# Attention with a routed mixture of experts on one core: the place of the output evictions on the queues of ScalarE and VectorE

## The chip, the cores and the metric

The kernel runs on one core of one Trainium2 chip. A core has five engines with a queue of instructions each: TensorE (PE in the profile, its weight loads PEld), VectorE (DVE), ScalarE (ACT), GpSimd (POOL) and SyncE (SP), which here only issues transfers. The metric is the time of one execution in microseconds (us); the time before is the median of three runs.

## The reference

Causal attention with a decaying bias over 8 batches, 8 heads, 576 positions and head size 64; then each of the 4608 tokens goes to the one of 8 experts with the highest logit, through two matrices with a ReLU between, and is scaled by its gate.

```python
scores = scale * np.matmul(q, k.transpose(0, 1, 3, 2))
...
attn = np.exp(scores)
attn = attn / (np.sum(attn, axis=-1, keepdims=True) + 1e-09)
...
x = np.ascontiguousarray(attn_out.transpose(0, 2, 1, 3)).reshape(B * S, H * D)
...
logits = x @ w_gate + modality_bias[modality_id]
e_idx = np.argmax(logits, axis=1)
...
for e in range(E):
    mask = e_idx == e
    ...
    h = np.maximum(x[mask] @ w1[e], 0.0)
    out[mask] = gate_w[mask, None] * (h @ w2[e])
```

Here x is 4608 x 512, w1 of one expert 512 x 1024, w2 of one expert 1024 x 512, all in 32-bit floats.

## The kernel before, in words

The first half of the time is the attention (class Attn), whose output rows are scattered into one list for each expert (Route). The second half is the experts (class Moe), in blocks. A block is 256 rows of one expert's list. There are 18 such blocks (6 from the table t2, 12 from t3); I count them from 0. After them come two short pieces of 64 rows each (`two`), and a loop over what is left, which the diff does not touch.

A block (`block`, then `second`) has these parts.

- Its expert's weights come as 8 tiles of 128 x 1024, four of w1 and four of w2, by SP into raw buffers (`fetch`, tiles wraw and wrbw; the buffers are few, and a transfer into one waits for its last reader). `parts` converts a raw tile: a cast to the matmul's reduced 32-bit type on ScalarE (L975), which is the high part, and on VectorE the raw value less that high part (L976), which is the low part. The converted tiles are called wca, wcb and wcc, by the pool that they come from. High and low parts are multiplied in three passes (`PASS1`, `PASS`), to keep the precision.
- Its rows come as tile xr, and `xt` turns them: two transposes on VectorE (L1067), a cast on ScalarE (L1069) and a subtraction on VectorE (L1070) for each half of xT. This is issued between the two halves of the block before.
- First half: 96 matmuls of 256 columns into hp (L1117), with four times a ReLU on ScalarE (L1119) and a subtraction on VectorE (L1120) that make hT.
- Second half: 48 matmuls of 512 columns into the two banks y (L1092).
- Eviction: y[0] times the gate on ScalarE (L1102), y[1] times the gate on VectorE (L1100), each into a tile ys, and a scatter of ys to the output's rows by POOL (L1103). Both evictions wait for the block's last matmuls.

While a block runs, `step` issues the fetches and conversions of the next block's eight tiles, one at a time: two before the block begins, and then one after each of the four steps of the first half and of the second. Which row stands where on an engine's queue is not the order of the code alone: the tile context's scheduler orders the rows of each engine, and `issue_after(i)` tells it that what follows must stand behind instruction i. Each engine then works its queue off in order. So a row that waits at the head of a queue holds up all rows behind it.

Of the kernel before, what the change touches and what calls it, by code (L numbers as in the profile page):

```python
# [7 lines left out]
F32 = mybir.dt.float32  # L8
# [3 lines left out]
AF = mybir.ActivationFunctionType  # L12
ALU = mybir.AluOpType
# [560 lines left out]
N2 = 6  # L574
WGP = (1, 2, 3, 4, 8)
PRI = 300
PRI2 = 900
PRI3 = 200
SCS = 5, 5, 4, 4
# [331 lines left out]
class Moe:  # L911
    def __init__(self, ctx, tc, R, w1, w2, ident, out):
        self.nc, self.tc, self.R, self.w1, self.w2, self.ident, self.out = tc.nc, tc, R, w1, w2, ident, out
        self.wa = ctx.enter_context(tc.tile_pool(name="mwa", bufs=1))
        self.wb = None
        self.n = 0
        self.last = [None] * 4
        self.hold = None
        self.late, self.stop = None, 1 << 30
        self.back = ()  # L920
        self.er = None

    def open(self, ctx):
        tc = self.tc
        self.my, self.mx, self.wr, self.wb, self.mp = (
            ctx.enter_context(self.tc.tile_pool(name=n, bufs=2, reuse_waits="tile")) for n in ("mys", "mmx", "mwr", "mwb", "mm"))
        self.R.tb = ctx.enter_context(tc.tile_pool(name="mtb", bufs=1, reuse_waits="tile"))
        self.ps = ctx.enter_context(tc.tile_pool(name="mps", bufs=2, space=PSUM, reuse_waits="tile"))
# [28 lines left out]
    def parts(self, raw, d, n, j, w=None):  # L957
        nc = self.nc
        m = (n - self.NA) % (self.NA + self.NB + self.NC)
        if w is not None:  # L960
            pass
        elif n < self.NA or self.NB <= m < self.NB + self.NA:
            w = self.wa.tile([P, 2, 1024], F32R, name="wca", bufs=self.NA)
        elif m < self.NB:
            w = self.wb.tile([P, 2, 1024], F32R, name="wcb", bufs=self.NB)
        else:
            w = self.wc.tile([P, 2, 1024], F32R, name=f"wcc{(m - self.NB - self.NA + 2) % self.NC}")
        n += 1
        with ExitStack() as after:
            for i in self.tr[1:] if 4 < n <= 8 else self.back:  # L970
                after.enter_context(self.tc.issue_after(i.ins))
            if n <= self.NA:
                nc.gpsimd.tensor_scalar(w[:, 0], raw, 1.0, 1.0, ALU.mult, ALU.mult)
            else:
                nc.scalar.copy(w[:, 0], raw)  # L975
            (nc.gpsimd if n in WGP else nc.vector).tensor_tensor(w[:, 1], raw, w[:, 0].bitcast(F32), ALU.subtract)  # L976
        return w, d

    def regs(self, tb, b):
# [103 lines left out]
    PASS = ((0, 0), (0, 1), (1, 0))  # L1083
    PASS1 = ((0, 0), (1, 0), (0, 1))

    def second(self, W, xg, oi, hT):
        nc = self.nc
        y = [self.ps.tile([P, 512], F32, name="y") for _ in range(2)]
        for f in range(8):
            for u in range(2):  # L1090
                for i, (a, c) in enumerate(self.PASS):
                    self.last[0] = nc.tensor.matmul(y[u], hT[:, a, f, P * u:P * u + P], W[4 + f // 2][:, c, 512 * (f % 2):512 * (f % 2) + 512],  # L1092
                                                    start=f == 0 and i == 0, stop=f == 7 and i == 2)
            if f % 2:
                self.step()
        for u in range(2):
            ys = self.my.tile([P, 512], F32, name="ys", bufs=3)
            gate = xg[1][:, u, 0:1]
            if u:
                self.last[1] = nc.vector.tensor_scalar(ys, y[u], gate, None, ALU.mult)  # L1100
            else:
                self.last[3] = nc.scalar.activation(ys, y[u], AF.Copy, scale=gate)  # L1102
            self.last[2] = nc.gpsimd.indirect_dma_start(  # L1103
                out=self.out, out_offset=bass.IndirectOffsetOnAxis(ap=oi[:, u:u + 1], axis=0),
                in_=ys, in_offset=None, bounds_check=4607, oob_is_err=False)

    def block(self, W, xg, oi, xT, mid):

        nc = self.nc
        hT = self.mp.tile([P, 2, 8, 256], F32R, name="hT", bufs=1)  # L1110
        for m in range(4):
            hp = self.ps.tile([P, 2, 256], F32, name="hp")
            for u in range(2):
                f = P * (2 * m + u)
                for k in range(4):
                    for i, (a, c) in enumerate(self.PASS1):
                        nc.tensor.matmul(hp[:, u], W[k][:, a, f:f + P], xT[:, c, k], start=k == 0 and i == 0, stop=k == 3 and i == 2)  # L1117
            hs = hT[:, 0, 2 * m:2 * m + 2]
            hi = nc.scalar.activation(hs, hp, AF.Relu)  # L1119
            lo = nc.vector.scalar_tensor_tensor(hT[:, 1, 2 * m:2 * m + 2], hp, 0.0, hs.bitcast(F32), ALU.max, ALU.subtract)  # L1120
            if self.late is not None:
                self.back = (hi, lo)
            self.step()
        mid()
        self.second(W, xg, oi, hT)

    def quads(self, xg, k):
        return xg[:, 0, :32].rearrange("p d h r -> p (d h r)")[:, k::4]
# [91 lines left out]
    def sums(self, o, W, parts, scale=1.0, after=()):  # L1220

        nc = self.nc
        n = len(parts)
        for i, (x, k, c0) in enumerate(parts):
            def low():
                nc.tensor.matmul(o[:64], x[:, :64], W[k][:, 1, c0:c0 + 512], start=False, stop=False)
            if i:
                low()
            self.last[0] = nc.tensor.matmul(o, x, W[k][:, 0, c0:c0 + 512], start=i == 0, stop=i == n - 1)
            if not i:  # L1230
                low()
        lo = self.wc.tile([64, 512], F32, name="ql", bufs=2)
        with ExitStack() as behind:
            for i in after:
                behind.enter_context(self.tc.issue_after(i.ins))
            self.last[3] = nc.scalar.activation(lo, o[64:], AF.Copy, scale=scale)
        return lo
# [70 lines left out]
    def run(self, lst, early=False, then=None, routed=None, half=None):  # L1308

        def pre(k):  # L1310
            tb, b, nu = getattr(self.R, lst[k][0]), lst[k][1], lst[k][2]
            if nu == 0:
                e, r = zip(*(self.regs(tb, b + q) for q in range(2)))
                self.stop = self.n + 14
            else:
                e, r = self.er if early and k == 0 else self.regs(tb, b)
            if early and k == 0:
                (xg, oi), x = self.first
            else:
                xg, oi = self.gather(tb, b, r, nu)  # L1320
                x = self.xt(xg, nu) if k == 0 else None
            W, self.more = self.weights(e, self.have if early and k == 0 else ()) if nu else self.weights2(e)
            for _ in range(0 if self.late is not None else 2 if k else 8):
                next(self.more, 0)
            return W, xg, oi, x
        with (self.tc.high_priority(offset=PRI) if early else ExitStack()):
            *nxt, nx = pre(0)
        if routed is not None:
            routed()
        for k in range(len(lst)):  # L1330
            cur, xT = nxt, nx
            if then is not None:
                then(k)
            if early and k == 0:
                self.stop = 8 + self.NB + 2
            if k + 1 < len(lst):
                *nxt, _ = pre(k + 1)
            def mid():
                if half is not None:
                    half(k)  # L1340
                if k + 1 < len(lst):
                    nxts.append(self.xt(nxt[1], lst[k + 1][2]))
            nxts = []
            with (self.tc.high_priority(offset=PRI) if early and k == 0 else ExitStack()):
                (self.two, self.quarter, self.block)[lst[k][2]](*cur, xT, mid)
            if early and k == 0:
                self.late, self.stop = self.more, 1 << 30
            else:
                while self.n < self.stop and next(self.more, 0) is None:
                    pass  # L1350
            self.back = ()
            nx = nxts[0] if nxts else None


def build(tc, qkv, s, mid, wg, mb, w1, w2, out):
    nc = tc.nc
    with ExitStack() as ctx:
# [36 lines left out]
        with ExitStack() as mctx:  # L1394
# [3 lines left out]
            def routed():  # L1398
                with ExitStack() as after:
                    for i in M.tr[1:]:  # L1400
                        after.enter_context(tc.issue_after(i.ins))
                    with tc.high_priority(offset=PRI2):
                        while next(bg[0][0]) != "mm":
# [64 lines left out]
```

## Time and profile before

| | us |
|---|---|
| three runs | 816.35, 816.20, 814.23; median 816.2 |
| profiled execution | 815.56 |
| its span, first to last instruction | 813.8 |
| mean granted clock of TensorE | 0.994 of full |
| first eviction of an expert block, last one | 400.35, 791.40 |

All rows are of the profiled execution, counted from the start of its span. A row of the timeline gives start, length, engine, line, operation, what is written from what is read, the tile sizes and how many; in a bracket, how long the engine had waited before it and for what. The waits are put down to what came last by the profile.

### The profile page before, as it was taken

What the parts mean: (1) busy time and instruction counts of PE and PEld (TensorE: products, weight loads), DVE (VectorE), ACT (ScalarE), POOL (GpSimd) and SP (SyncE); (2) the same over time, 40 slices, a digit from 0 to 9 for tenths busy, and PEclk for the clock granted to TensorE, in tenths of its full rate; (3) what the DMA queues carried; (4) which work ended last, traced back from release to release, by engine and by line L of the source; (5) the groups of instructions that cost most, each with busy time, mean ns of one, the idle gap of its engine ahead of it and who ended that gap; (6) DMA issues with size and microseconds to landing.
All of it is one profiled execution on the core that took longest, in us unless ns stands there. A gap on an engine that the chain in (4) does not pass through costs nothing. (4 is left out here: it accounts for less than half of the span.)

```text
span 813.8 us, 16745 instructions
## 1 busy us (share of the span) xinstructions
PE 796.1 (98%) x5548; PEld 681.1 (84%) x5548; DVE 577.9 (71%) x1441; ACT 526.4 (65%) x1194; POOL 364.2 (45%) x385
## 2 busy tenths in 40 slices
PE   7999999999999999999999999899999999999997
PEld 6778888888878888887888998798889998988884
DVE  7666667667666677768779695677787776777664
ACT  6788778887878788785554544555555555455553
POOL 8959777988699867984601001100000010001000
PEclk9999999999999999999999999999999999999999
DMA  7665556776567665749888977577778777778750
GB/s 240 175 197 184 181 185 196 230 236 194 166 186 215 220 178 171 233 151 256 292 278 279 321 253 278 177 253 231 249 254 260 252 242 254 262 256 249 257 182 29
DMA packets 88133, 181.16 MB, mean 223 GB/s; under 512 B 13753, under 2 KB 33081, under 8 KB 87918
## 3 DMA queue, kind: packets, MB, share of 16 engines
q1 hardware_dynamic: 82206, 160.03, 62.6%
q0 software_dynamic: 5840, 20.06, 6.3%
q8 instruction: 44, 0.72, 0.4%
q14 instruction: 43, 0.35, 0.1%
HBM read 143.59 MB, written 26.80 MB: 209 GB/s over the span
## 5 line engine op out<-in xcount | busy, mean ns | idle before, releaser
L1103 POOL DMA_INDIRECT out<-ys,oi x36 | 38.7, 1075 | 356.9 <-ACT ys L1102 267.6
L396 DVE CUSTOM_DVE_ANT_0 pe<-sp,mk 128x512 f32<-128x512 f32 (+3 forms) x256 | 122.4, 488 | 99.6 <-PE sp L394 91.2
L416 ACT ACTIVATE pe<-pe,mx 128x512 f32<-128x512 f32 (+3 forms) x256 | 144.4, 565 | 16.8 <-DVE mx L396 14.2
L433 PE MATMUL pt<-ident,pe 128*128 128x128 f32 x640 | 110.6, 278 | 0.8 <-ACT PT L437 0.5
L437 ACT COPY PT<-pt 128x512 f32<-128x512 f32 (+1 forms) x192 | 97.2, 509 | 20.3 <-PE pt L433 20.3
L372 PE MATMUL sp<-KA,QH 128*128 128x256 f32 (+2 forms) x256 | 102.4, 402 | 2.4 <-POOL KA L236 2.4
L1119 ACT ACTIVATE hT<-hp 128x512 fp32r<-128x512 f32 x72 | 43.1, 599 | 92.9 <-PE hp L1117 89.9
L474 PE MATMUL o<-PT,V 128*64 128x320 f32 (+4 forms) x896 | 100.7, 364 | 1.1 <-DVE PT L451 1.1
L474 PEld LDWEIGHTS o<-PT,V 128*64 128x64 f32 x896 | 58.6, 136 | 47.8 <-issue 14.7
L1117 PE MATMUL hp<-xT,wcb 128*128 128x256 f32 x648 | 89.9, 282 | 0.2 <-DVE wcb L976 0.2
L326 POOL TENSOR_TENSOR KA<-rawk,KA 64x576 fp32r<-64x576 f32 x62 | 87.2, 1424 | 0.2
L433 PEld LDWEIGHTS pt<-ident,pe 128*128 128x128 f32 x640 | 75.9, 143 | 13.6 <-issue 5.3
L326 POOL TENSOR_TENSOR QL<-rawq,QH 64x576 fp32r<-64x576 f32 x62 | 86.8, 1415 | 0.2
L394 PE MATMUL sp<-KB,QL 76*128 76x256 f32 (+2 forms) x256 | 85.4, 338 | 0.0
L1117 PEld LDWEIGHTS hp<-xT,wcb 128*128 128x128 f32 x648 | 83.4, 188 | 1.0 <-DVE wcb L976 0.4
L1120 DVE SCALAR_TENSOR_TENSOR hT<-hp,hT 128x512 fp32r<-128x512 f32 x72 | 49.5, 688 | 46.1 <-ACT hT L1119 46.0
L1092 PE MATMUL y<-wcb,hT 128*128 128x512 f32 x336 | 80.9, 396 | 0.0
L1117 PE MATMUL hp<-xT,wca 128*128 128x256 f32 x528 | 75.9, 284 | 2.4 <-ACT wca L975 1.5
L1092 PEld LDWEIGHTS y<-wcb,hT 128*128 128x128 f32 x336 | 62.6, 188 | 14.5
L1117 PEld LDWEIGHTS hp<-xT,wca 128*128 128x128 f32 x528 | 68.5, 192 | 4.0 <-ACT wca L975 1.9
L1117 PE MATMUL hp<-xT,wcc 128*128 128x256 f32 x456 | 65.4, 282 | 1.9 <-DVE wcc L976 1.2
L1092 PE MATMUL y<-wcc,hT 128*128 128x512 f32 x264 | 63.1, 394 | 0.0
(290 smaller groups left out, 1624.7 us busy)
## 6 DMA issues: line engine op xcount, KB each, us to landing
wrbw<-in_w SPq DMA_DIRECT2D x104, 512.0 KB
wraw<-in_w SPq DMA_DIRECT2D x56, 512.0 KB
rawq<-in_qkv SPq DMA_DIRECT2D x31, 576.0 KB
rawk<-in_qkv SPq DMA_DIRECT2D x31, 576.0 KB
V<-in_qkv SPq DMA_DIRECT2D x32, 320.0 KB
KB<-KA SPq DMA_DIRECT2D x62, 144.0 KB
xr<-lists SPq DMA_DIRECT2D x68, 128.0 KB
lists<-z SPq DMA_DIRECT2D x8, 576.0 KB
```

The lines of the kernel that those rows point to most:

```text
L326: self.last = nc.gpsimd.tensor_tensor(o, i, h, ALU.subtract).ins
L372: self.pe.append(self.nc.tensor.matmul(sp[:, :nn], QH[:, q0:q0 + P], self.KA[u][:, ab, :nn], start=True, stop=False).ins)
L394: self.pe.append(nc.tensor.matmul(sp[:, :nn], QL[:EXT, q0:q0 + P], KB[:EXT, ab, :nn], start=False, stop=True).ins)
L396: ins = nc.vector.tensor_tensor_reduce(out=t[:, :n], in0=sp[:, :n], in1=self.mk[:, 512 - n:512], scale=-0.125, scalar=3.0e38, op0=ALU.add, ...
L416: self.act = nc.scalar.activation(t[:, :n], t[:, :n], AF.Exp, bias=m, scale=-1.0, accum_out=st["sums"][:, o:o + 1]).ins
L433: self.pe.append(nc.tensor.transpose(out=pt[:, o:o + P], in_=pe[:, P * j:P * j + P], identity=self.ident).ins)
L437: cp(w[:, :, :, v:v + P], pt[:, :n * (1 + both)].rearrange("p (a j q) -> p a j q", a=1 + both, q=P))
L474: m = nc.tensor.matmul(o[r, f - q0:q1 - q0], V[:, ab, j, :], PT[:, ab, PTS * j + f if j < 4 else PTW - 64:PTS * j + q1 if j < 4 else PTW], ...
L1092: self.last[0] = nc.tensor.matmul(y[u], hT[:, a, f, P * u:P * u + P], W[4 + f // 2][:, c, 512 * (f % 2):512 * (f % 2) + 512], start=f == 0 ...
L1117: nc.tensor.matmul(hp[:, u], W[k][:, a, f:f + P], xT[:, c, k], start=k == 0 and i == 0, stop=k == 3 and i == 2)
L1119: hi = nc.scalar.activation(hs, hp, AF.Relu)
L1120: lo = nc.vector.scalar_tensor_tensor(hT[:, 1, 2 * m:2 * m + 2], hp, 0.0, hs.bitcast(F32), ALU.max, ALU.subtract)
```

## The change

`parts` now keeps, for each weight tile in the order of conversion, the pair of its two instructions (cast on ScalarE, subtraction on VectorE) in the list `conv`. `second` orders the eviction of y[0] (ScalarE) behind the cast, and that of y[1] (VectorE) behind the subtraction, of the tile `8 * k + 8 + 3`: block k + 1 begins with tile 8 * k + 8, so this is its fourth. Only the place on the queue is set; each eviction is on the same engine as the instruction that it is ordered behind.

```diff
+AHEAD = 3
...
+        self.conv, self.high = [], None
...
             else:
-                nc.scalar.copy(w[:, 0], raw)
-            (nc.gpsimd if n in WGP else nc.vector).tensor_tensor(w[:, 1], raw, w[:, 0].bitcast(F32), ALU.subtract)
+                self.high = nc.scalar.copy(w[:, 0], raw).ins
+            self.conv.append((self.high, (nc.gpsimd if n in WGP else nc.vector).tensor_tensor(w[:, 1], raw, w[:, 0].bitcast(F32), ALU.subtract).ins))
...
-    def second(self, W, xg, oi, hT):
+    def second(self, W, xg, oi, hT, ahead):
...
             gate = xg[1][:, u, 0:1]
-            if u:
-                self.last[1] = nc.vector.tensor_scalar(ys, y[u], gate, None, ALU.mult)
-            else:
-                self.last[3] = nc.scalar.activation(ys, y[u], AF.Copy, scale=gate)
+            with self.tc.issue_after(self.conv[ahead][u]):
+                if u:
+                    self.last[1] = nc.vector.tensor_scalar(ys, y[u], gate, None, ALU.mult)
+                else:
+                    self.last[3] = nc.scalar.activation(ys, y[u], AF.Copy, scale=gate)
...
-        self.second(W, xg, oi, hT)
+        self.second(W, xg, oi, hT, ahead)
...
-                (self.two, self.quarter, self.block)[lst[k][2]](*cur, xT, mid)
+                (self.two, self.quarter, self.block)[lst[k][2]](*cur, xT, mid, *([8 * k + 8 + AHEAD] if lst[k][2] == 2 else []))
```

In 16 of the 18 blocks the evictions stood behind the next block's fourth tile already, and the rows of ScalarE and VectorE are in the same order before and after. They move in blocks 4 and 5. On POOL and SP no row moves; on TensorE a few matmuls of the first half of block 5, within the first twenty, change places among themselves. The code has three lines more, so the line numbers are 2 or 3 higher after the change.

ScalarE at the end of block 4, from the casts of xT for block 5 on; the casts to wcc and wcb are block 5's tiles in their order. Before:

```order
L1069 CAST xT<-tp 128x512 x2
L975 CAST wcc_6763<-wrbw 128x1024
L975 CAST wcc_6768<-wrbw 128x1024
L1102 ACTIVATE ys<-y,tg 128x512
L975 CAST wcc_6801<-wraw 128x1024
L975 CAST wcb<-wrbw 128x1024 x2
L975 CAST wcb<-wraw 128x1024
```

And the same place after:

```order
L1071 CAST xT<-tp 128x512 x2
L977 CAST wcc_6763<-wrbw 128x1024
L977 CAST wcc_6768<-wrbw 128x1024
L977 CAST wcc_6801<-wraw 128x1024
L977 CAST wcb<-wrbw 128x1024
L1105 ACTIVATE ys<-y,tg 128x512
L977 CAST wcb<-wrbw 128x1024
```

The eviction moved back behind the third and the fourth tile. On VectorE it moved likewise, there by three rows, since it stood behind the first subtraction.

ScalarE at the end of block 5; the four casts to wca are block 6's first four tiles. Before:

```order
L975 CAST wcb<-wrbw 128x1024
L1069 CAST xT<-tp 128x512
L1102 ACTIVATE ys<-y,tg 128x512
L1069 CAST xT<-tp 128x512
L975 CAST wca<-wraw 128x1024
L975 CAST wca<-wrbw 128x1024 x2
L975 CAST wca<-wraw 128x1024
```

And after:

```order
L977 CAST wcb<-wrbw 128x1024
L1071 CAST xT<-tp 128x512 x2
L977 CAST wca<-wraw 128x1024
L977 CAST wca<-wrbw 128x1024 x2
L977 CAST wca<-wraw 128x1024
L1105 ACTIVATE ys<-y,tg 128x512
```

Here the eviction moved back behind the second half of xT and all four casts.

VectorE at the same place, from the transposes of block 6's rows on. Before:

```order
L1067 STREAM_TRANSPOSE tp<-xr 128x512
L1070 TENSOR_TENSOR xT<-tp,xT 128x512
L1100 TENSOR_SCALAR ys<-y,tg 128x512
L1070 TENSOR_TENSOR xT<-tp,xT 128x512
L976 TENSOR_TENSOR wca<-wraw,wca 128x1024
L976 TENSOR_TENSOR wca<-wrbw,wca 128x1024 x2
L976 TENSOR_TENSOR wca<-wraw,wca 128x1024
L976 TENSOR_TENSOR wcc_7140<-wrbw,wcc_7140 128x1024
```

And after:

```order
L1069 STREAM_TRANSPOSE tp<-xr 128x512
L1072 TENSOR_TENSOR xT<-tp,xT 128x512 x2
L978 TENSOR_TENSOR wca<-wraw,wca 128x1024
L978 TENSOR_TENSOR wca<-wrbw,wca 128x1024 x2
L978 TENSOR_TENSOR wca<-wraw,wca 128x1024
L1103 TENSOR_SCALAR ys<-y,tg 128x512
L978 TENSOR_TENSOR wcc_7140<-wrbw,wcc_7140 128x1024
```

The eviction moved back behind one subtraction of xT and four of weights.

More of the change, by code (lines that the diff above doesn't have):

```diff
@@ L1105, in second, with block @@
                 in_=ys, in_offset=None, bounds_check=4607, oob_is_err=False)
-    def block(self, W, xg, oi, xT, mid):
+    def block(self, W, xg, oi, xT, mid, ahead):
         nc = self.nc
```

## The prediction

> **What bounds the kernel now.** I read the page first, then the times of the evictions, then the rows of TensorE, ScalarE and VectorE around the two places where the order of the queues changes.
>
> ```profile
> PE 796.1 (98%) x5548; PEld 681.1 (84%) x5548; DVE 577.9 (71%) x1441; ACT 526.4 (65%) x1194; POOL 364.2 (45%) x385
> PEclk9999999999999999999999999999999999999999
> ```
>
> TensorE is busy for 98% of the span, and its granted clock is 0.9 or more in every fortieth of it. The change takes no matmul away. So time can be won only where TensorE waits or where its clock drops. The other engines have idle time; what they do matters only if TensorE waits for it.
>
> The next rows are the first half of the eviction (ScalarE, L1102) of the expert blocks that I count as 2 to 7 (the first is 0): start, length, and in the bracket ScalarE's idle time before it.
>
> ```profile
> 445.66 0.69 ACT L1102 ACTIVATE ys<-y,tg 128x512 f32<-128x512 f32 x1 [1.80 <-PE y L1092]
> 468.00 0.69 ACT L1102 ACTIVATE ys<-y,tg 128x512 f32<-128x512 f32 x1 [1.73 <-PE y L1092]
> 490.59 0.69 ACT L1102 ACTIVATE ys<-y,tg 128x512 f32<-128x512 f32 x1 [2.82 <-PE y L1092]
> 515.35 0.69 ACT L1102 ACTIVATE ys<-y,tg 128x512 f32<-128x512 f32 x1 [5.41 <-PE y L1092]
> 542.48 0.69 ACT L1102 ACTIVATE ys<-y,tg 128x512 f32<-128x512 f32 x1 [1.98 <-PE y L1092]
> 565.05 0.69 ACT L1102 ACTIVATE ys<-y,tg 128x512 f32<-128x512 f32 x1 [3.01 <-PE y L1092]
> ```
>
> Each of these starts when TensorE has finished the first half of a block's output, so the distance of two is the time of a block. From the second row on the distances are 22.59, 24.76, 27.13 and 22.57 us, for blocks with the same 96 + 48 matmuls. Blocks 5 and 6 are longer than their neighbours' mean of 22.58 by 2.18 and 4.55 us, **together 6.73 us**. TensorE's rows show where (xN is a count, the bracket the wait ahead):
>
> ```profile
> 491.09 1.11 PE L1117 MATMUL hp<-xT,wcc 128*128 128x256 f32 x8
> 493.22 0.97 PE L1117 MATMUL hp<-xT,wcc 128*128 128x256 f32 x6 [1.03 <-DVE wcc L976]
> 494.36 0.50 PE L1117 MATMUL hp<-xT,wcc 128*128 128x256 f32 x2 [0.16 <-DVE wcc L976]
> ...
> 495.50 0.50 PE L1117 MATMUL hp<-xT,wcb 128*128 128x256 f32 x2 [0.17 <-DVE wcb L976]
> ...
> 505.31 10.71 PE L1092 MATMUL y<-wcb,hT 128*128 128x512 f32 x45
> 517.51 0.50 PE L1117 MATMUL hp<-xT,wca 128*128 128x256 f32 x2 [1.50 <-ACT wca L975]
> 518.77 0.97 PE L1117 MATMUL hp<-xT,wca 128*128 128x256 f32 x6 [0.76 <-DVE wca L976]
> 519.91 6.62 PE L1117 MATMUL hp<-xT,wca 128*128 128x256 f32 x40 [0.16 <-DVE wca L976]
> 526.37 0.86 PE L1092 MATMUL y<-wcc,hT 128*128 128x512 f32 x3
> ```
>
> Both blocks begin with waits for their own converted weight tiles: 1.03 + 0.16 + 0.17 = 1.36 us in block 5, 1.50 + 0.76 + 0.16 = 2.42 us in block 6. In the second place a lower clock follows. In the windows below the columns are busy time (instructions) of PE, PEld, DVE, ACT and POOL, then granted clock, DMA share and GB/s:
>
> ```profile
> 516.00:520.00 4.00, 1.58 (x10) 1.16 (x9) 3.86 (x5) 4.00 (x6) 1.17 (x2) 1.00 0.30 74
> 520.00:522.00 2.00, 2.00 (x10) 1.71 (x11) 2.00 (x2) 2.00 (x3) 1.84 (x1) 0.63 0.85 289
> 522.00:524.00 2.00, 2.00 (x12) 2.00 (x11) 2.00 (x3) 0.19 (x1) 0.00 (x0) 0.52 1.03 386
> ```
>
> At 0.63 and 0.52 of its clock TensorE lost 2 x 0.37 + 2 x 0.48 = 1.70 us. Waits and clock give 1.36 + 2.42 + 1.70 = 5.48 us. The other 1.25 us up to 6.73 I put down to the lengths shown for the matmuls just ahead of a wait, whose ends are modelled.
>
> Why were the weights late? ScalarE's rows at the two places:
>
> ```profile
> 485.76 2.01 ACT L975 CAST wcc<-wrbw 128x1024 fp32r<-128x1024 f32 x2
> ...
> 491.18 1.04 ACT L975 CAST wcc<-wraw 128x1024 fp32r<-128x1024 f32 x1
> ...
> 509.35 0.59 ACT L1069 CAST xT<-tp 128x512 fp32r<-128x512 f32 x1 [2.31 <-DVE tp L1067]
> ...
> 515.94 0.58 ACT L1069 CAST xT<-tp 128x512 fp32r<-128x512 f32 x1
> 516.40 1.06 ACT L975 CAST wca<-wraw 128x1024 fp32r<-128x1024 f32 x1
> 517.35 2.00 ACT L975 CAST wca<-wrbw 128x1024 fp32r<-128x1024 f32 x2
> ```
>
> The eviction stands at the head of ScalarE's queue and waits for TensorE, 2.82 and 5.41 us by the brackets above. Queued behind it are casts of the next block: at 491 us two of its first four tiles, at 516 us half of xT and all four. They run as soon as it is gone, without a wait of their own. VectorE shows the same:
>
> ```profile
> 486.85 1.23 DVE L976 TENSOR_TENSOR wcc<-wrbw,wcc 128x1024 fp32r<-128x1024 f32 x1 [0.26 <-ACT wcc L975]
> 491.29 0.75 DVE L1100 TENSOR_SCALAR ys<-y,tg 128x512 f32<-128x512 f32 x1 [3.21 <-PE y L1092]
> 491.96 1.21 DVE L976 TENSOR_TENSOR wcc<-wrbw,wcc 128x1024 fp32r<-128x1024 f32 x1
> 493.09 1.22 DVE L976 TENSOR_TENSOR wcc<-wraw,wcc 128x1024 fp32r<-128x1024 f32 x1
> ...
> 509.26 1.10 DVE L1067 STREAM_TRANSPOSE tp<-xr 128x512 f32<-128x512 f32 x1
> ...
> 516.05 0.75 DVE L1100 TENSOR_SCALAR ys<-y,tg 128x512 f32<-128x512 f32 x1 [5.11 <-PE y L1092]
> ```
>
> **The change part by part.** No instruction is added or removed. In 16 of the 18 blocks the evictions already stand behind the fourth tile, and the order on ScalarE and VectorE stays: nothing gained or lost. In blocks 4 and 5 the evictions move back behind two and behind four more tiles. The queues of SP and POOL keep their order. The conversions that the evictions now stand behind are on the same engine.
>
> Boundary at 491 us. The third cast can follow the second at 487.8 (485.76 + 2.01), and the fourth ends near 489.8, ahead of the eviction's 490.59, which is thus not late. VectorE's subtractions run on from 486.85 at a pace of 1.13 us (491.96 to 493.09): the fourth ends near 486.85 + 3 x 1.13 + 1.23 = 491.5. VectorE's eviction comes 0.2 us later than before. TensorE takes a new tile's low part with every sixth matmul: by the rows' counts the waits stand behind 2 and 2 + 6 in block 6. The fourth tile's comes with the 21st, 20 x 0.12 = 2.4 us after 491.09, at 493.5, so 2 us to spare. (0.12 us a matmul is block 4's pace, below: 11.40 us for 96.) The whole 2.18 us goes.
>
> Boundary at 516 us, in the old times. The second transpose ends at 510.36, the second xT cast near 511.0, four weight casts at 0.95 (516.40 to 517.35) near 514.8: ahead of the eviction at 515.35. VectorE's first subtraction can start near 512.2 and the fourth ends near 516.8. VectorE's eviction, due at 516.05, is **0.75 us late**. Behind it stand conversions for the second half of block 6 and, on POOL, the scatter of these rows. The bank that it empties is written again only after 2 + 6 + 40 = 48 matmuls (the row at 526.37), 5.7 us on; this cover hides the delay, which would cost 0.75 us without it. The fourth tile's low part is wanted 2.4 us after 516.02 (505.31 + 10.71), at 518.4, and is done at 516.8: 1.6 us to spare. Were VectorE's chain two subtractions later (2.3 us), TensorE would wait 0.7 us. So the new order costs between 0 and 0.7 us; I take 0, which is what the rows give. With the waits gone I let the clock stay at 1.00. So the 4.55 us go too.
>
> ```profile
> 468.50 1.22 PE L1117 MATMUL hp<-xT,wcb 128*128 128x256 f32 x9
> ...
> 479.90 8.57 PE L1092 MATMUL y<-wca,hT 128*128 128x512 f32 x36
> ```
>
> Have the raw tiles landed that early? A window without transfers, the last issues, and two full windows tell:
>
> ```profile
> 478.00:482.00 4.00, 4.00 (x27) 3.61 (x26) 3.94 (x10) 2.33 (x3) 0.00 (x0) 1.00 0.09 22
> 471.75 0.33 SPq L950 DMA_DIRECT2D wrbw<-in_w  x1
> 498.10 0.40 SPq L950 DMA_DIRECT2D wraw<-in_w  x1
> 498.00:502.00 4.00, 4.00 (x34) 3.86 (x32) 1.38 (x2) 0.72 (x2) 0.00 (x0) 1.00 0.97 278
> 502.00:506.00 4.00, 4.00 (x33) 3.88 (x32) 1.92 (x2) 2.03 (x3) 0.00 (x0) 1.00 0.89 346
> ```
>
> The last of block 5's first four was issued at 471.75, and from 478 to 482 the engines moved only 22 GB/s: all had landed, 6 us ahead of 487.8. Block 6's first four are issued from 498.10 on; up to 506 the engines moved 4 x 278 + 4 x 346 = 2.5 MB, more than four tiles of 0.52 MB. So they are there near 506, and are first wanted near 511. They even start earlier now, since raw buffers come free earlier: block 5's second subtraction ends near 489.2, not 493.2.
>
> **The sum.** The profiled execution took 815.56 us (span 813.8, 1.76 around it). Less 2.18 and 4.55 that is 808.83. The median of the three runs is 816.2, 0.64 above it; less 6.73 that is 809.47. I take **809.0 us**, nearer to the profile's own. The gain is at least the 5.48 us that the rows name. At most it is what the shortest block gives, 468.00 - 445.66 = 22.34: 2.42 + 4.79 = 7.21 us.
>
> **The rivals.**
>
> 1. The clock drop is not the waits' doing and stays: the gain is 6.73 - 1.70 = 5.03 us, the time 810.5. For it: eight matmuls ran between the waits, and 1.36 us of waiting at 491 us brought no drop. Against it: the drop follows the longest waits of the expert blocks within microseconds, and the next row shows none in 153 us without a wait. [...] Chance 0.08.
>
> ```profile
> 527.00:680.00 153.00, 153.00 (x976) 138.44 (x975) 113.31 (x130) 81.76 (x105) 13.10 (x13) 1.00 0.79 257
> ```
>
> 2. Only the first boundary is mended, because at 516 us transfers or VectorE are as late as the eviction was: 815.56 - 2.18 = 813.4. Against it are the 2.5 MB moved by 506. Chance 0.04.
> 3. The waits move on, later blocks being bound by transfers, and the time is given back: 815.6. For it: a DMA share of 0.97 and 1.03 in single windows. Against it: the row above, 0.79 over seven blocks in which TensorE never waits. Chance 0.03.
> 4. Slower: the fourth transfer lands late, and the eviction queued behind its cast waits along, which it did not before. Cast and subtraction (1.05 + 1.22) must end before the 21st matmul, so a landing 0.1 us past the boundary is borne; each microsecond more at both places costs two. At 5 us past it costs 2 x 4.9 = 9.8 us: 815.56 - 6.73 + 9.8 = 818.6. It passes today's time by 0.3% from (6.73 + 2.45) / 2 + 0.1 = 4.7 us on. Against it: landings at 482 and 506. Chance 0.03.
>
> That the change does nothing is excluded by the rows of order: the evictions move at exactly the two long blocks.
>
> **How the numbers follow.** The forecast has 0.82; with rival 1 faster has 0.90. Rivals 2 and 3 end about within 0.3% (2.45 us, which is about what a measurement of this kernel can tell from no change): 0.07. Slower: 0.03. The range takes in the forecast and rival 1. At the bottom stands the largest gain, 815.56 - 7.21 = 808.35, less the 1.33 by which the lowest of the three runs (814.23) lies under the profiled one: 807.0. At the top stands rival 1 with 0.7 us of waiting and the 0.64 us of the median: 811.8.
>
> **What would show it.** Right: evictions of blocks 4, 5 and 6 at distances of 22.3 to 22.8 us; no wait on wcc or wca at the two boundaries; no clock under 1.00 near 515; block 5's third cast near 487.8; everything from block 7 on 6.7 us earlier. Wrong: a cast there that waits for a DMA, a wait at a later boundary that was not there, a low clock without a wait.

## The result, and the profile after

The changed kernel takes **808.25 us** (median of four runs, 807.68 to 808.87); the kernel before took 815.45 us in the same comparison. The ratio is 0.9913, with a 95% interval from 0.9895 to 0.9930. The forecast was 809.0 us in a range from 807.0 to 811.8.

The evictions on ScalarE in the profile after, for blocks 3 to 7 again (the line is now L1105):

```profile
467.88 0.69 ACT L1105 ACTIVATE ys<-y,tg 128x512 f32<-128x512 f32 x1 [1.73 <-PE y L1094]
490.47 0.69 ACT L1105 ACTIVATE ys<-y,tg 128x512 f32<-128x512 f32 x1 [0.93 <-PE y L1094]
513.09 0.69 ACT L1105 ACTIVATE ys<-y,tg 128x512 f32<-128x512 f32 x1 [0.57 <-PE y L1094]
535.15 0.69 ACT L1105 ACTIVATE ys<-y,tg 128x512 f32<-128x512 f32 x1 [1.98 <-PE y L1094]
557.73 0.69 ACT L1105 ACTIVATE ys<-y,tg 128x512 f32<-128x512 f32 x1 [3.01 <-PE y L1094]
```

The distances are 22.59, 22.62, 22.06 and 22.58 us. Block 5 went from 24.76 to 22.62, block 6 from 27.13 to 22.06: 2.14 + 5.07 = 7.21 us. That is nearly the whole gain: the last eviction comes 7.23 us earlier (784.17 for 791.40). The first one starts 1.00 us later (401.35 for 400.35), and what is left is the first distance, 1.24 us shorter, and small differences. TensorE's rows at the two places have no bracket any more:

```profile
490.96 2.18 PE L1120 MATMUL hp<-xT,wcc 128*128 128x256 f32 x17
...
503.05 10.71 PE L1094 MATMUL y<-wcb,hT 128*128 128x512 f32 x45
513.60 5.61 PE L1120 MATMUL hp<-xT,wca 128*128 128x256 f32 x48
519.04 0.86 PE L1094 MATMUL y<-wcc,hT 128*128 128x512 f32 x3
519.74 5.62 PE L1120 MATMUL hp<-xT,wca 128*128 128x256 f32 x48
525.19 5.04 PE L1094 MATMUL y<-wcc,hT 128*128 128x512 f32 x21
```

And the whole list of TensorE's waits from 395 to 800 us (total, times, longest) has one row left, where it had five:

```profile
PE hp L1120 <- DVE hT L1123: 0.7, 1, 0.7
```

ScalarE and VectorE do at the two places what the order of the queues lets them do:

```profile
487.54 1.05 ACT L977 CAST wcc<-wraw 128x1024 fp32r<-128x1024 f32 x1
488.49 1.05 ACT L977 CAST wcb<-wrbw 128x1024 fp32r<-128x1024 f32 x1
...
508.62 1.05 ACT L977 CAST wca<-wraw 128x1024 fp32r<-128x1024 f32 x1
509.58 1.99 ACT L977 CAST wca<-wrbw 128x1024 fp32r<-128x1024 f32 x2
511.47 1.04 ACT L977 CAST wca<-wraw 128x1024 fp32r<-128x1024 f32 x1
```

```profile
490.14 1.22 DVE L978 TENSOR_TENSOR wcb<-wrbw,wcb 128x1024 fp32r<-128x1024 f32 x1
491.27 0.75 DVE L1103 TENSOR_SCALAR ys<-y,tg 128x512 f32<-128x512 f32 x1
...
513.12 1.22 DVE L978 TENSOR_TENSOR wca<-wraw,wca 128x1024 fp32r<-128x1024 f32 x1
514.25 0.75 DVE L1103 TENSOR_SCALAR ys<-y,tg 128x512 f32<-128x512 f32 x1
```

The casts stand in the time in which ScalarE had waited for TensorE: its wait ahead of the two evictions is 0.93 us for 2.82, and 0.57 for 5.41. At the second boundary VectorE's eviction starts at 514.25, about 0.5 us after TensorE's last matmul into y (503.05 + 10.71 = 513.76). TensorE does not wait for it: the next matmuls into y, at 519.04, have no bracket.

### The profile page after: what moved, and what is told of

It is laid out like the page before. It is cut to its first block, busy times and chain, and to the rows that moved or that the text cites. A ratio compares the mean times of both kernels' runs of the same rounds, so it can differ in the third digit from the quotient of the medians.

```text
span 806.6 us, 16745 instructions
## 1 busy us (share of the span) xinstructions
PE 793.5 (98%) x5548; PEld 680.1 (84%) x5548; DVE 577.1 (72%) x1441; ACT 526.7 (65%) x1194; POOL 364.0 (45%) x385
## 5 line engine op out<-in xcount | busy, mean ns | idle before, releaser
L1120 PE MATMUL hp<-xT,wca 128*128 128x256 f32 x528 | 73.3, 279 | 0.0
```

## The experiments

The theory: at each of the two boundaries the eviction held the head of a queue while it waited for TensorE; the conversions behind it were late by that wait, and TensorE then waited for them. The rivals: the lower clock is a thing of its own; only one engine's half of the eviction matters; a late eviction costs as much as it brings. The times of blocks 5 and 6 (distances of ScalarE's evictions in each run's profile) tell them apart better than whole times do, as will be seen. All of them, with the lowest clock that a window of two to five microseconds shows near the second boundary; a time without a word beside it is that of one execution:

| run | block 5, us | block 6, us | lowest clock | time, us |
|---|---|---|---|---|
| before / profiled again | 24.76 / 24.73 | 27.13 / 26.97 | 0.52 / 0.50 | 815.56 / 817.28 |
| after / again / third | 22.62 / 22.61 / 22.62 | 22.06 / 22.07 / 22.07 | 1.00 in all | 808.25 / 808.37 / 808.33 (medians) |
| only block 4's evictions moved / again | 22.62 / 22.62 | 26.22 / 26.50 | 1.00 / 0.55 | 812.87 (median) / 812.37 |
| only block 5's moved | 24.75 | 22.07 | 1.00 | 811.41 (median) |
| only VectorE's half moved | 23.90 | 26.30 | 0.50 | 813.96 |
| block 5's behind the first tile | 22.62 | 24.60 | 1.00 | 811.23 |
| block 5's behind the second tile | 22.61 | 23.48 | 1.00 | 809.78 |
| block 5's behind the last tile | 30.21 | 14.62 | 1.00 | 808.05 |

**One boundary alone, and the clock.** The order is applied to block 4's evictions only (tile 43 is the fourth of block 5); then, with 51 for 43, to block 5's only.

```diff
-            with self.tc.issue_after(self.conv[ahead][u]):
+            with (self.tc.issue_after(self.conv[ahead][u]) if ahead == 43 else ExitStack()):
```

> Only the evictions of block 4 are ordered behind the fourth tile; those of block 5 stand where they stood before the change. Theory (each boundary's loss comes from the eviction at the head of the queue, and the two are independent): the boundary at 491 us has no wait, and block 5 takes 22.6 us instead of 24.8; block 6 still takes 27.1, with waits of about 1.5 and 0.8 us and a clock near 0.5 for some 3.4 us after them. Time 2.1 to 2.2 us under the kernel before, ratio about 0.9973. Rival (the clock drop is not the waits' doing but comes at a fixed time): the drop stays near 520 us in absolute time instead of moving 2.1 us earlier with the wait. Rival (one boundary's loss moves to the next): block 6 takes more than 28 us and the time is that of before.

Measured: ratio 0.9977 (0.9966 to 0.9989). Block 5 takes 22.62 us, as expected. Block 6 takes 26.22, and here the expectation was wrong in one point: the waits are there, the drop of the clock is not. It is also under the 28 us of the second rival: the first boundary's loss does not move to the next. TensorE's rows at the start of block 6, and the windows over them (columns as in the prediction):

```profile
515.74 0.50 PE L1120 MATMUL hp<-xT,wca 128*128 128x256 f32 x2 [1.49 <-ACT wca L977]
516.99 0.96 PE L1120 MATMUL hp<-xT,wca 128*128 128x256 f32 x6 [0.76 <-DVE wca L978]
518.13 0.97 PE L1120 MATMUL hp<-xT,wca 128*128 128x256 f32 x6 [0.17 <-DVE wca L978]
519.26 0.97 PE L1120 MATMUL hp<-xT,wca 128*128 128x256 f32 x6 [0.17 <-DVE wca L978]
520.40 3.46 PE L1120 MATMUL hp<-xT,wca 128*128 128x256 f32 x28 [0.17 <-DVE wca L978]
```

```profile
516.00:518.00 2.00, 1.20 (x8) 0.80 (x7) 2.00 (x3) 2.00 (x3) 0.00 (x0) 1.00 0.38 134
518.00:520.00 2.00, 1.71 (x12) 1.51 (x12) 2.00 (x3) 2.00 (x3) 1.96 (x1) 1.00 0.95 245
```

The first waits are the ones of before (1.50 and 0.76), the clock is 1.00, and block 6 still takes 4.15 us more than the 22.07 of the other runs. So the waits alone cost 4.15 us, and the drop in the kernel before only the rest of its 5.07, 0.9 us. The brackets of these rows add up to 2.76 only; the starts show the loss better: from the second row on, six matmuls take 1.13 or 1.14 us, which is the pace of VectorE's subtractions, where six without a wait take 0.68 (6 x 0.114, worked out further below). To see whether the drop belongs to one kernel and not to the other, both were profiled once more.

> Only block 4's evictions moved, profiled once more. Theory (the drop is a matter of phase): 26.2 us for block 6 with a clock of 1.00, or 26.3 to 27.2 with a drop; block 5 22.6. Rival (without the first boundary's wait the clock never drops): 26.2 us and 1.00 again. A drop here refutes that rival; none leaves it open.

> The kernel before, profiled once more. In its first profile block 6 took 27.13 us with a half clock for some 3.4 us; with only block 4's evictions moved it took 26.22 us with the same waits and a clock of 1.00. [...] Rival (the drop belongs to the kernel before, through both waits together): a drop again and 27.1 us.

Measured: a drop in both. With only block 4's evictions moved, the same kernel that had none shows

```profile
516.00:518.00 2.00, 1.88 (x9) 1.89 (x10) 2.00 (x3) 2.00 (x3) 0.84 (x1) 0.59 0.33 23
518.00:520.00 2.00, 2.00 (x12) 2.00 (x11) 2.00 (x3) 1.54 (x2) 1.19 (x1) 0.55 0.99 383
```

and block 6 takes 26.50 us: 0.28 for a drop that takes 2 x 0.41 + 2 x 0.45 = 1.72 us of clock. So neither the two boundaries together nor this kernel decides whether the clock drops: the same waits do it in one execution and not in another. Nor does a fixed time: the drops start 0.9 to 3.0 us behind the end of the first wait. The sum of the waits does not decide it either (by the brackets 2.76 us without a drop, 2.42 in the kernel before with one). What decides it, the phase that one expectation names or another thing, these runs do not show.

In the first profile of the kernel before the granted clock changes only at whole multiples of 3.413 us from one another: 505.17 us of full clock (148 of them) lie between a half clock near the start and the drop at 520.52, the drop lasts one, and 286.72 us of full clock (84) follow it. Two windows of that grid there:

```profile
517.11:520.52 3.41, 2.09 (x13) 1.68 (x14) 3.32 (x4) 3.41 (x5) 0.89 (x2) 1.00 0.43 108
520.52:523.93 3.41, 3.41 (x16) 3.12 (x16) 3.41 (x4) 1.67 (x2) 1.32 (x1) 0.50 1.00 370
```

In the first TensorE is busy for 2.09 us at a clock of 1.00, in the second for all of its 3.41 us at 0.50. Whether the waits of the two executions of one kernel lie differently on such a grid is not shown.

A drop also costs less than the clock that it takes. While it lasts, TensorE's matmuls stand where it would have waited for the next tile; the brackets of 0.17 are gone from this profile:

```profile
516.12 7.13 PE L1120 MATMUL hp<-xT,wca 128*128 128x256 f32 x46 [0.76 <-DVE wca L978]
```

Full price is paid only behind the last tile's wait, 4.66 us after block 6's first matmul by the rows above (520.40 - 515.74). Of the four drops that the profiles show 0, 0.27, 1.08 and 1.74 us lie behind it (only VectorE's half moved; this profile; the kernel before again; its first profile). At half clock that is a cost of 0, 0.14, 0.54 and 0.87 us, as an estimate; over the 26.22 us without a drop they took 0.08, 0.28, 0.75 and 0.91.

> Only the evictions of block 5 are ordered behind the fourth tile. Theory: block 5 keeps its 24.8 us with waits of 1.36 us in sum and a clock of 1.00; block 6 takes 22.1 us, as with the whole change, without a wait and without a drop of the clock. Time 5.0 to 5.1 us under the kernel before, ratio about 0.9938. Rival (the clock drop needs both waits, or is not caused by the waits): a window below 1.00 between 505 and 530 us although the waits at 516 are gone; then block 6 takes 23.8 us.

Measured: block 5 24.75 us, with the old waits and a clock of 1.00; block 6 22.07, with no wait and no drop. The two boundaries are independent, and the rival (a drop without the waits at 516) did not come. The time, 0.9952 (0.9935 to 0.9968), is 3.6 us under the median of before, where the distances say 5.06; the interval reaches from 2.6 to 5.3 us and so takes that in. The last block, which the edit does not touch, took 23.58 us in this profile and 22.94 in the first two; it varies so between executions of one kernel (22.94, 23.42 and 23.43 for the changed kernel).

**One engine's half alone.**

```diff
-            with self.tc.issue_after(self.conv[ahead][u]):
+            with (self.tc.issue_after(self.conv[ahead][u]) if u else ExitStack()):
```

> Only the half of the eviction on VectorE is ordered; the half on ScalarE stands where it stood before the change, at both places. Theory (the casts queued behind ScalarE's eviction are what is late, the subtractions follow them): at 491 us the wait for the second tile goes, those for the third and fourth stay, and block 5 takes 23.6 to 24.0 us; at 516 us all four casts are still late, block 6 takes 26.5 to 27.2 us with the clock drop. Time 0.7 to 1.7 us under the kernel before. Rival (VectorE's half is what holds up TensorE): most of the 7 us is gained, time under 810.

Measured: block 5 23.90 us; block 6 26.30, with a drop of the clock, 0.2 us under the range expected, since the drop cost only 0.08 us here (26.30 less 26.22); one run of 813.96 us. The rival falls: with ScalarE's half in its old place, most of the loss stays. At the first boundary TensorE no longer waits for the second tile, since that cast always stood ahead; its first wait is for the third:

```profile
493.52 0.62 PE L1120 MATMUL hp<-xT,wcc 128*128 128x256 f32 x3 [0.62 <-DVE wcc L978]
```

The other half alone was not run.

**How far behind.** Block 5's evictions behind the first tile of block 6, and behind the second (1 for 0 in the diff):

```diff
-                (self.two, self.quarter, self.block)[lst[k][2]](*cur, xT, mid, *([8 * k + 8 + AHEAD] if lst[k][2] == 2 else []))
+                (self.two, self.quarter, self.block)[lst[k][2]](*cur, xT, mid, *([8 * k + 8 + (0 if k == 5 else AHEAD)] if lst[k][2] == 2 else []))
```

> As the changed kernel, but the evictions of block 5 stand behind the first tile of block 6 instead of the fourth, so half of xT and one tile are converted ahead, three tiles wait. Theory: casts 2 to 4 start when ScalarE's eviction is done near 513.7 us, the last subtraction ends near 518.3 where its matmul is due at 516.0: TensorE loses 2.4 us in waits of under 1.3 us each, and block 6 takes 24.5 us if the clock stays at 1.00, 26.2 if it drops as it did before. [...] Rival (xT alone was the late part): block 6 takes 22.1 to 22.5.

> As the changed kernel, but the evictions of block 5 stand behind the second tile of block 6. Theory: casts 3 and 4 start near 513.7 us, the fourth subtraction ends near 517.3 against a matmul due at 516.0: TensorE loses 1.3 us, block 6 takes 23.3 to 23.5 us, and the clock stays at 1.00 as it did at 491 us before the change with a similar loss. Rival (two tiles ahead are enough, the fourth's place is slack): 22.1 us.

Measured: 24.60 us (forecast 24.5 without a drop) and 23.48 (23.3 to 23.5), the clock at 1.00 in both. With no tile ahead (and half of xT behind too) block 6 took 26.22 us without a drop, with one 24.60, with two 23.48, with four 22.07. So the conversions let past the eviction bring their share, and two are not enough: the fall from two to four is still 1.4 us. Three were not tried.

**The other way: too far behind.** Block 5's evictions behind the eighth and last tile of block 6 (7 for 0 in the diff above).

> As the changed kernel, but the evictions of block 5 stand behind the last tile of block 6, some 8 us after the output is finished. The scheduler then puts all 96 matmuls of block 6's first half ahead of the first into y, where three stood in the middle; a few rows of later blocks change places too. Theory (a late eviction is covered by the matmuls ahead of the next write of its bank): block 6 takes 22.0 to 22.6 us without a wait on y, and the time is within 1 us of the changed kernel's. Rival (a late eviction costs): TensorE waits before the first matmul into y for an eviction, 1 us or more.

Measured: 808.05 us in one run. The evictions come at 520.16 and 521.64, some 8 us after the output was there. So ScalarE's distances shift to 30.21 and 14.62 us, but their sum, 44.83, is that of the changed kernel (22.62 + 22.06 = 44.68) but for 0.15 us.

```profile
513.08 11.21 PE L1120 MATMUL hp<-xT,wca 128*128 128x256 f32 x96
524.13 11.32 PE L1094 MATMUL y<-wcc,hT 128*128 128x512 f32 x48
```

The scheduler put all 96 matmuls ahead of the first into y, and that at 524.13 has no wait. The rival falls for this order of rows. It does so with a queue of TensorE that was reordered to suit; what a late eviction costs ahead of matmuls that keep their place was not tried. Rows of later blocks moved too: block 11 takes 23.46 us for 22.46, with a wait of 0.80 us for hT, and block 13 22.66 for 23.58, without one. So the whole time says less than the sum for the two blocks.

**The same fault once more?** One wait is left in the changed kernel: in block 13, which takes 23.58 us, TensorE waits 0.69 us for hT. Its subtraction stands on VectorE behind the turning of the next block's rows. That turning was ordered behind block 13's first hT subtraction.

```diff
+            if m == 0:
+                self.first_lo = lo.ins
...
-                    nxts.append(self.xt(nxt[1], lst[k + 1][2]))
+                    with (self.tc.issue_after(self.first_lo) if k in TURNS else ExitStack()):
+                        nxts.append(self.xt(nxt[1], lst[k + 1][2]))
```

with `TURNS = (13,)`, beside the changed kernel on the same chip, twice.

> As the changed kernel, and in block 13 the turning of block 14's rows (two transposes, two casts, two subtractions) is ordered behind block 13's first hT subtraction. In the changed kernel block 13 takes 23.58 us and TensorE waits there 0.69 us for hT, whose subtraction stands behind those transposes on VectorE. Theory (the same mechanism, a row at the head of a queue that is not urgent): block 13 takes 22.5 to 22.9 us, the wait on hT goes, and the time is 0.7 to 1.1 us under the changed kernel's, 807.2 to 807.6. Rival (the turning was needed there): a wait on xT at the start of block 14 takes its place, and the time is the changed kernel's.

> The changed kernel again, on the same chip and against the same runs of the kernel before as the run with the turning moved. Theory: 0.9905 to 0.9920 of the kernel before, and the eviction distances of the first profile again (block 5 22.6, block 6 22.1, block 13 23.6 us). Rival (block 6's 22.06 us was chance): block 6 takes 22.4 to 22.6.

> The kernel with the turning of block 14's rows moved, again, beside the changed kernel in the same job. Theory: block 13 takes 22.6 us, and the median is 0.7 to 1.1 us under the changed kernel's of this job. Rival (what is won in block 13 is lost by its end): the medians differ by less than 0.4 us.

> The changed kernel, as the partner of the run with the turning moved. Theory: ratio 0.990 to 0.993 against the kernel before; blocks 5, 6 and 13 at 22.6, 22.1 and 23.6 us. Rival (the difference of the two kernels is chance): its median is within 0.4 us of the other's.

Measured: block 13 took 22.62 and 22.63 us, against 23.60 and 23.58 in the partner's profiles. TensorE's rows there, without a wait:

```profile
672.34 8.70 PE L1121 MATMUL hp<-xT,wcc 128*128 128x256 f32 x72
680.88 0.86 PE L1095 MATMUL y<-wcb,hT 128*128 128x512 f32 x3
```

So 0.95 to 0.98 us are won in that block, and no new wait was seen. The times do not show it: 807.42 against 808.37 us in the first comparison, as expected, but 809.07 against 808.33 in the second, where 0.7 to 1.1 us less was expected. The ratios to the kernel before are 0.9913 and 0.9924, then 0.9922 and 0.9924; the first 0.9924 lies just over its expected 0.9905 to 0.9920. The intervals are some 0.003 wide, and the 0.95 us of the first comparison are 0.0012. A wait removed is shown, a faster kernel is not.

## Why the prediction was right, point by point

- *The bound is TensorE's waiting, and the two long blocks hold the loss.* Right. The gain is 2.14 + 5.07 us in just these blocks; of the other distances all but the first (21.17 for 22.41 us) agree with those of before to 0.2 us. The first varies with the same kernel too: it is 21.35 us in the second profile of before.
- *The cause is the eviction at the head of the queue.* Shown by the run of each boundary alone, and, for the second boundary, by the row of one, two and four tiles ahead.
- *First boundary, 2.18 us.* Measured 2.14. The third cast starts at 487.54 (487.8 forecast), the fourth ends at 489.54 (489.8), VectorE's fourth subtraction at 491.36 (491.5).
- *Second boundary, 4.55 us.* The mechanism was right, the size was not: 5.07. **The mis-sized term is the time that block 6 has without waits.** I took its neighbours' mean, 22.58, and it is 22.06 or 22.07 in each of six profiles without a wait. So the sign "distances of 22.3 to 22.8 us" failed for block 6, on the fast side. TensorE's timeline of the kernel before had the rows for it:

```profile
527.06 5.62 PE L1117 MATMUL hp<-xT,wca 128*128 128x256 f32 x48
532.51 0.85 PE L1092 MATMUL y<-wcc,hT 128*128 128x512 f32 x3
```

  These are the 48 matmuls of block 6 behind the waits: 5.45 us, or 0.114 each, where block 4 has 0.119. Over 96 that is 0.5 us. The upper bound, 7.21 us, was taken from another short block as 2.42 + 4.79; that the gain came out at just this sum, as 2.14 + 5.07, is luck. The time of 809.0 lay 0.75 us over the measured one, mainly for this term and for the 0.17 by which it was set above the sum of 808.83.
- *1.36 + 2.42 of waits and 1.70 of clock as the parts of the loss.* The clock's part was too large. At the second boundary the waits alone cost 4.15 us (26.22 less 22.07), of which the rows show 2.76 as brackets; a drop on top cost 0.08 to 0.91 us in the four profiles that have one, not 1.70. The 1.25 us that no part covered are of the kind that the starts showed: the brackets are too short for the waits. The lost clock was counted as if nothing lay beside it, though TensorE would have waited for part of that time. The forecast came near because it went by distances and not by these parts.
- *Rival 1, the drop is not the waits' doing and stays.* Half right. Without the waits at 516 us it was seen in none of seven profiles (three of the changed kernel, two with the turning moved, only block 5's evictions moved, and block 5's behind the last tile), so it did not stay. But the waits alone do not decide it either: with the same ones block 6 took 26.22 us at a clock of 1.00 in one execution and 26.50 with a clock down to 0.55 in another. What decides it is not shown. The four drops that the windows show take 1.70 to 1.72 us of clock each, which at half clock lasts 3.4 us. In the kernel before, profiled again, that is 2 x (0.09 + 0.50 + 0.27) = 1.72:

```profile
520.00:522.00 2.00, 1.25 (x7) 1.05 (x8) 2.00 (x3) 2.00 (x3) 0.37 (x1) 0.91 0.20 76
522.00:524.00 2.00, 2.00 (x10) 2.00 (x11) 2.00 (x3) 2.00 (x3) 1.66 (x1) 0.50 0.85 323
524.00:526.00 2.00, 2.00 (x15) 2.00 (x14) 2.00 (x2) 0.01 (x1) 0.00 (x0) 0.73 1.01 379
```

  The longest single wait ahead of each of the four was 1.50 us; with one of 1.49 (only block 4's evictions moved) the clock stayed at 1.00.
- *The delay of VectorE's eviction, 0.75 us, is covered.* Right: about 0.5 us late, without a wait behind it.
- *Transfers.* The rivals on late transfers did not come: no cast at the two places waits for one, and TensorE's waits did not move on to later blocks. The transfers start earlier, as was said: block 6's first at 493.99 for 498.10. The last two tiles of block 5 were issued over 5.49 us from 488.11, and now:

```profile
487.98 1.53 SPq L954 DMA_DIRECT2D wrbw<-in_w  x2
```

## What to carry to other kernels

A row that waits at the head of an in-order queue costs what stands behind it (here 2.14 us with two casts behind ScalarE's wait of 2.82 us, and 5.07 with four and half of xT behind one of 5.41). If it is not urgent itself, put it behind the urgent rows, and count how many of those fit into its wait. Compare the times of equal stages first: two long ones among eighteen gave the place here, and the gain to 0.5 us; but take the reference for each from its own undisturbed rows where there are any. Where a lower clock lies beside waits, don't add the two: the four drops here took 1.70 to 1.72 us of clock each and cost 0.08 to 0.91, since TensorE would have waited for part of that time anyway.

## What the runs showed of the hardware that was not expected

- Blocks in the middle of the experts repeat to 0.01 to 0.2 us from one profile to the next where no row moved, but block 1 varies from 21.04 to 22.41 us and the last block from 22.94 to 23.59, and the first eviction starts at 399.71 to 406.13 us. In the three profiles of the changed kernel (808.33, 812.27 and 808.33 us) these ends make the spread: against the first of them, the longest has its first eviction 2.8 us later, block 1 1.2 us longer and the last block 0.5 us longer.
- Whether TensorE's clock drops after a given wait changed from one execution of a kernel to the next (only block 4's evictions moved: block 6 took 26.22 us at a clock of 1.00, and 26.50 with two windows at 0.59 and 0.55). In the first profile of the kernel before the clock changed on a grid of 3.413 us, with 505.17 us (148 of them) of full clock between two half clocks.
- Equal matmuls run at slightly different pace in different blocks: 0.114 us each in block 6 and 0.119 in block 4, at a clock of 1.00 and without waits. What makes the difference was not tried.
